# A new order for the first 250 of 1101 steps of a gated SSM-convolution and MLP-mixer kernel on one core

## The chip, the core and the metric

The kernel runs on one core of one Trainium2 chip. The metric is the device time of the whole program in microseconds (us). The kernel before took 228.67 us, the median of three runs (228.26 to 228.98).

The engines of the core are named as the profile names them: PE (TensorE, matmuls; PEld its weight loads), DVE (VectorE), ACT (ScalarE), POOL (GpSimd) and SP (SyncE, which here only issues DMAs). Each works through its own instruction queue in order.

## What is computed

All tensors are bf16; S = 2048 rows, D = 640 columns, F = 1536.

```python
g = sigmoid((x * gate_w).sum(-1))                     # x = A_q
k_shift = sum(k_pad[t:t+S] * shift_k[:, 3-t] for t in range(4))
kv = k_shift * v
y = causal_convolution_by_fft(kv, ssm_k) + kv * ssm_D
a = x * y
h = gelu(layernorm(x) @ w1)
hs = concat(shift(h[:, :160], +1), shift(h[:, 160:320], -1),
            shift(h[:, 320:480], +2), shift(h[:, 480:], -2)) @ w2
x1 = x + hs
b = x1 + gelu(layernorm(x1) @ w3) @ w4
out = g * a + (1 - g) * b
```

## The kernel before, in words

**Layout.** The 2048 rows lie as 128 partitions of 16 rows each (t = 0 to 15), cut in four chunks of four rows t. A chunk of x, k or v is 128 x 2560 bf16, 640 KB. The columns come in five blocks of 128.

**Order.** Every engine's instructions are written out by hand: ORDER is a list of 1101 names such as `mlp1.0.2:1`. The name is a function with its arguments, the number behind the colon is the step of it that is emitted (a generator's next part, or an element of a list of closures). So the list gives each engine its queue, and each queue is simply the list's steps for that engine in the list's order. Letters at the end of a name (`AVA`) say for each part whether ACT (A) or DVE (V) does the evacuation. SLOTS is the second hand-written table: for each ring of buffers (`c`: the eight PSUM banks; `row`: four buffers of a chunk; `gt`, `gq`, `xt` and others) it lists which buffer each allocation gets.

**The stage that the change touches**, up to the first matmul of w2 (`w2.0:0`, step 250):

- `warm` (L224): 23 matmuls of zeros. `consts0`, `pow0`, `row_order` (L220 to L255): constants, a first power on POOL, and the row list for gathers. `f4_table`, `f1_table`, `t2_table` (L280 to L325): sine tables; their arguments are made on DVE, the sine is taken on ACT, and t2_table's part 1 adds a 128 x 1024 table on POOL (L322).
- `load_x0`, `load_x` (L189 to L193), `load_w1` by halves (L195), `k_load.c:0` (L562): loads on SP's queue. `v_load.c` (L575): a gather of v's chunk c on POOL's queue (L173), into KV.
- `x_stats.c` (L667): sums for the layer norm, by bn_stats on DVE (V, L686) or by a Square and a Copy pass on ACT (A, L680 and L682), then scalars on DVE and the reciprocal root on POOL (L658). `x_norm.c` (L629) scales the rows. `x_turn.c` turns the chunk: by PE transposes with evacuations (letters; L620, L361 or L363) for chunks 0 and 1, by one transposing DMA (D, L653) for chunks 3 and 2.
- `k_load.c:1` to `:6`: the same transposes for k, in three banks (two of 8 blocks, one of 4), into KT; odd numbers are PE, even ones the evacuation. `k_wrap` (L567) makes the last three rows of KT again, shifted by a partition.
- `mlp1.c.u` (L701): five matmuls of 128 x 512 for chunk c and column group u, then Gelu on ACT. u = 0 and 1 need W1's first half, 2 and 3 the second, 4 the mixed columns that `w1_mixed` copies. `h_shift.c` (L750): copies on POOL for the row shifts.
- `tap.k` (L578): 76 matmuls that give k_shift of column block k in four PSUM banks; then for each quarter e the product with v: V is one DVE product straight from PSUM (L606), A a copy to yk on ACT (L600) and a product on DVE (L603). Each quarter's product takes all 16 rows of KV.
- `step1.KV.c` (L411): the first transform of a chunk of kv, five pairs of matmuls (L424), ten evacuations, two sends to DRAM on SP (L438). Each matmul reads only the column blocks that it covers. `load_h` (L178) loads ssm_k, `h_transpose` turns it.

From step 250 on follow w2, the rest of the transforms, w3 and w4, and the output.

Of the kernel before, what the change touches and what calls it, by code (L numbers as in the profile page):

```python
# [41 lines left out]
def kernel(  # L42
# [837 lines left out]
    def step4(t1, ev):  # L880
# [91 lines left out]
        "x_norm.1.VVVV:2 "
        "v_load.2:0 "
        "k_load.0.AAV:0 "
        "f1_table:1 "
        "mlp1.0.2:0 "
        "mlp1.0.3:0 "
        "x_norm.1.VVVV:3 "
        "v_load.0:0 "
        "k_load.1.AVV:0 "  # L980
        "k_load.2.VAV:6 "
        "mlp1.0.0:0 "
        "load_x.2:0 "
        "x_stats.3.VVAA:2 "
        "x_turn.1.VVV:0 "
        "x_turn.1.VVV:4 "
        "mlp1.0.1:0 "
        "x_stats.3.VVAA:3 "
        "x_turn.1.VVV:1 "
        "k_load.2.VAV:4 "  # L990
        "x_stats.3.VVAA:4 "
        "x_stats.3.VVAA:5 "
        "k_load.0.AAV:3 "
        "x_turn.1.VVV:5 "
        "mlp1.0.3:1 "
        "x_stats.3.VVAA:6 "
        "x_turn.1.VVV:2 "
        "v_load.3:0 "
        "x_turn.1.VVV:3 "
        "k_load.1.AVV:3 "  # L1000
        "w1_mixed:0 "
        "v_load.1:0 "
        "mlp1.0.0:1 "
        "x_stats.2.VVAA:0 "
        "mlp1.0.2:1 "
        "k_load.0.AAV:1 "
        "mlp1.0.1:1 "
        "x_stats.3.VVAA:7 "
        "k_load.0.AAV:5 "
        "mlp1.1.2:0 "  # L1010
        "x_norm.3.VVVV:0 "
        "x_norm.3.VVVV:1 "
        "k_load.0.AAV:4 "
        "load_cj:0 "
        "k_load.0.AAV:2 "
        "mlp1.1.2:1 "
        "x_norm.3.VVVV:2 "
        "x_norm.3.VVVV:3 "
        "x_stats.2.VVAA:1 "
        "k_load.1.AVV:5 "  # L1020
        "mlp1.0.4:0 "
        "k_load.1.AVV:4 "
        "mlp1.0.4:1 "
        "k_load.1.AVV:1 "
        "d_fold:0 "
        "mlp1.1.4:0 "
        "x_turn.3.D:0 "
        "kv_consts:0 "
        "x_stats.2.VVAA:2 "
        "mlp1.1.0:0 "  # L1030
        "k_load.2.VAV:2 "
        "k_wrap:0 "
        "k_load.1.AVV:6 "
        "mlp1.1.4:1 "
        "k_load.0.AAV:6 "
        "x_stats.2.VVAA:3 "
        "t2_table:0 "
        "load_w2:0 "
        "mlp1.1.3:0 "
        "k_load.1.AVV:2 "  # L1040
        "tap.3.VAVA:0 "
        "mlp1.1.0:1 "
        "x_stats.2.VVAA:4 "
        "h_shift.1:0 "
        "mlp1.1.3:1 "
        "tap.4.VAAV:0 "
        "x_stats.2.VVAA:5 "
        "tap.3.VAVA:1 "
        "tap.3.VAVA:3 "
        "tap.3.VAVA:5 "  # L1050
        "h_shift.0:0 "
        "mlp1.1.1:0 "
        "tap.4.VAAV:7 "
        "x_stats.2.VVAA:6 "
        "tap.3.VAVA:4 "
        "tap.4.VAAV:1 "
        "load_h.2:0 "
        "tap.3.VAVA:7 "
        "z_cols:0 "
        "mlp1.1.1:1 "  # L1060
        "load_gw:0 "
        "tap.4.VAAV:5 "
        "tap.4.VAAV:3 "
        "mlp1.3.1:0 "
        "tap.3.VAVA:2 "
        "x_stats.2.VVAA:7 "
        "x_norm.2.AVVV:0 "
        "mlp1.3.1:1 "
        "mlp1.3.4:0 "
        "tap.4.VAAV:2 "  # L1070
        "mlp1.3.0:0 "
        "x_norm.2.AVVV:1 "
        "tap.4.VAAV:8 "
        "x_norm.2.AVVV:2 "
        "x_norm.2.AVVV:3 "
        "h_shift.0:1 "
        "tap.4.VAAV:6 "
        "tap.3.VAVA:6 "
        "mlp1.3.4:1 "
        "tap.4.VAAV:4 "  # L1080
        "mlp1.3.0:1 "
        "tap.2.AVAA:0 "
        "x_turn.2.D:0 "
        "h_shift.3:0 "
        "tap.0.AVAA:0 "
        "tap.2.AVAA:3 "
        "tap.2.AVAA:7 "
        "tap.2.AVAA:5 "
        "tap.3.VAVA:8 "
        "mlp1.3.3:0 "  # L1090
        "tap.0.AVAA:3 "
        "h_shift.0:2 "
        "tap.0.AVAA:5 "
        "tap.2.AVAA:8 "
        "h_shift.3:1 "
        "mlp1.3.2:0 "
        "tap.0.AVAA:4 "
        "tap.2.AVAA:6 "
        "tap.0.AVAA:1 "
        "mlp1.3.3:1 "  # L1100
        "tap.0.AVAA:6 "
        "tap.1.VAVA:0 "
        "tap.0.AVAA:7 "
        "tap.1.VAVA:5 "
        "tap.1.VAVA:1 "
        "tap.2.AVAA:4 "
        "mlp1.3.2:1 "
        "load_h.1:0 "
        "mlp1.2.2:0 "
        "tap.0.AVAA:8 "  # L1110
        "tap.2.AVAA:1 "
        "tap.1.VAVA:7 "
        "h_shift.1:1 "
        "tap.0.AVAA:2 "
        "load_h.3:0 "
        "mlp1.2.3:0 "
        "tap.1.VAVA:2 "
        "tap.1.VAVA:3 "
        "tap.2.AVAA:2 "
        "step1.KV.3.AAAVAVAAAV:9 "  # L1120
        "tap.1.VAVA:8 "
        "tap.1.VAVA:6 "
        "mlp1.2.2:1 "
        "mlp1.2.3:1 "
        "tap.1.VAVA:4 "
        "step1.KV.3.AAAVAVAAAV:11 "
        "step1.KV.3.AAAVAVAAAV:3 "
        "step1.KV.3.AAAVAVAAAV:10 "
        "step1.KV.3.AAAVAVAAAV:12 "
        "h_shift.0:3 "  # L1130
        "step1.KV.3.AAAVAVAAAV:13 "
        "step1.KV.3.AAAVAVAAAV:5 "
        "mlp1.2.4:0 "
        "step1.KV.3.AAAVAVAAAV:6 "
        "load_h.4:0 "
        "step1.KV.3.AAAVAVAAAV:0 "
        "step1.KV.3.AAAVAVAAAV:4 "
        "step1.KV.3.AAAVAVAAAV:14 "
        "h_shift.1:2 "
        "step1.KV.2.AVAVAVAAAA:6 "  # L1140
        "z_rows:0 "
        "z_rows:1 "
        "step1.KV.3.AAAVAVAAAV:2 "
        "step1.KV.3.AAAVAVAAAV:7 "
        "load_h.0:0 "
        "step1.KV.1.VAVAAAVVAA:0 "
        "step1.KV.3.AAAVAVAAAV:8 "
        "step1.KV.2.AVAVAVAAAA:8 "
        "step1.KV.3.AAAVAVAAAV:1 "
        "step1.KV.2.AVAVAVAAAA:3 "  # L1150
        "z_rows:2 "
        "mlp1.2.1:0 "
        "mlp1.2.1:1 "
        "h_shift.3:2 "
        "step1.KV.3.AAAVAVAAAV:16 "
        "step1.KV.1.VAVAAAVVAA:1 "
        "step1.KV.3.AAAVAVAAAV:15 "
        "mlp1.2.0:0 "
        "load_w4.0:0 "
        "load_w4.2:0 "  # L1160
        "h_transpose.0.VV:2 "
        "step1.KV.2.AVAVAVAAAA:5 "
# [905 lines left out]
```

## Time and profile before

| | us |
|---|---|
| three runs | 228.26, 228.67 (median), 228.98 |
| the profiled execution | 229.4 |
| its span, first to last instruction | 227.6 |
| busy: PE, PEld | 217.3, 121.4 |
| busy: DVE, ACT, POOL | 185.1, 171.6, 37.8 |
| DMA moved over the span | 57.61 MB, mean 253 GB/s |

A row of the profile names a line of the kernel, an engine, an operation, and `out<-in` by the program's names; `x` is a count. In rows of groups, busy us and mean ns of one stand behind the bar, then the idle time of the engine just before them and what ended it. In rows of the timeline the first two numbers are start and length in us from the span's start. In the chain of waits each piece is start, length, engine, tile and line. A DMA's row ends with the us from its issue to its landing. The granted PE clock was 1.00 in every stage quoted.

### The profile page before, as it was taken

The numbers are of one execution on the slowest core, as the hardware profiler recorded it, in microseconds if no ns is written. First come the engines' busy times: TensorE is split into PE (matmuls) and PEld (weight loads), VectorE is DVE, ScalarE is ACT, GpSimd is POOL, SyncE is SP. The second block draws the span as 40 slices with busy tenths as digits, with TensorE's granted clock in tenths as the row PEclk, the third lists the DMA queues.
The fourth block names the chain that finished last, engine by engine and source line by source line (L and its number), as shares of the span: only waits on it lengthen the run. The fifth ranks groups of instructions, "written<-read, shape, count | busy, mean of one in ns | idle before, by whom it ended". The sixth has DMA issues, their size and how long they took to land.

```text
span 227.6 us, 6057 instructions
## 1 busy us (share of the span) xinstructions
PE 217.3 (95%) x2428; PEld 121.4 (53%) x2428; DVE 185.1 (81%) x447; ACT 171.6 (75%) x341; POOL 37.8 (17%) x91
## 2 busy tenths in 40 slices
PE   8989988799999997999999999999999999999994
PEld 3647545337855553334665544555533547657762
DVE  7999996977889968981899997989999941439994
ACT  4999986869899978999987597976989450266450
POOL 4247247806000331300510000000000000000000
PEclk9999999999999999999999999999999999999999
DMA  6999999888999899997799590593694779418915
GB/s 247 398 386 306 265 259 162 256 340 292 384 350 411 285 206 287 347 397 232 252 147 370 134 260 17 127 334 121 78 313 172 234 264 365 196 29 322 319 75 183
DMA packets 41802, 57.61 MB, mean 253 GB/s; under 512 B 18478, under 2 KB 34478, under 8 KB 41518
## 3 DMA queue, kind: packets, MB, share of 16 engines
q1 hardware_dynamic: 41198, 54.60, 76.8%
q0 software_dynamic: 576, 2.62, 3.3%
q8 instruction: 19, 0.31, 0.6%
q14 instruction: 9, 0.07, 0.1%
HBM read 34.93 MB, written 18.35 MB: 234 GB/s over the span
## 4 chain that ended last, share of the span: by engine, by line
PE 73%; ACT 14%; DMA 6%; DVE 4%; issue 1%; ACTq 0%
PE ps L868 23%; PE ps L841 22%; PE psm L708 5%; PE psw L789 5%; PE ps L466 4%; PE ps L894 4%; ACT stg L361 4%; DMA S_h<-stg 3%; PE ps L513 3%; PE ps L424 2%; ACT HT L711 2%; PE pst L391 2%; DMA S_x<-stg 2%; ACT KT L361 1%; PE psk L591 1%
## 5 line engine op out<-in xcount | busy, mean ns | idle before, releaser
L841 PE MATMUL ps<-x1t,W 128*128 128x512 bf16 x240 | 56.1, 380 | 0.1
L868 PEld LDWEIGHTS <-gt 128*128 128x128 bf16 x384 | 36.2, 98 | 17.8 <-issue 3.0
L845 ACT ACTIVATE gt<-ps 128x512 bf16<-128x512 f32 x48 | 27.6, 609 | 19.0 <-PE ps L868 10.6
L841 PEld LDWEIGHTS <-W 128*128 128x128 bf16 x240 | 21.8, 98 | 28.2 <-issue 5.5
L361 ACT CAST stg<-ps 128x512 bf16<-128x512 f32 x55 | 28.8, 608 | 5.3 <-PE ps L424 3.4
L868 PE MATMUL ps<-W4a,gt 128*128 128x320 bf16 (+2 forms) x160 | 27.1, 300 | 0.0
L868 PE MATMUL ps<-W4b,gt 128*128 128x320 bf16 (+2 forms) x160 | 27.0, 300 | 0.0
L871 DVE SCALAR_TENSOR_TENSOR X<-ps,OMG,X 128x320 bf16<-128x320 f32 (+2 forms) x32 | 17.2, 547 | 11.9 <-PE ps L868 11.7
L789 PE MATMUL psw<-WP,HT 128*128 128x320 bf16 x116 | 21.4, 300 | 1.3 <-ACT stg L361 1.3
L361 ACT CAST gs<-ps 128x320 bf16<-128x320 f32 x41 | 15.6, 440 | 8.8 <-PE ps L513 4.8
L708 PE MATMUL psm<-xt,WN 128*128 128x512 bf16 x80 | 19.1, 380 | 1.8 <-ACT xt L361 0.9
L363 DVE CAST XS<-ps 128x512 bf16<-128x512 f32 x19 | 12.5, 685 | 6.9 <-PE ps L466 6.9
L363 DVE CAST stg<-ps 128x512 bf16<-128x512 f32 x25 | 15.9, 684 | 2.1 <-PE ps L424 2.1
L361 ACT CAST hs<-ps 128x512 bf16<-128x512 f32 x28 | 15.0, 605 | 1.4 <-PE ps L466 1.4
L792 DVE SCALAR_TENSOR_TENSOR X<-psw,X 128x320 bf16<-128x320 f32 x32 | 14.5, 487 | 1.7 <-PE psw L789 1.5
L789 PEld LDWEIGHTS <-HT 128*128 128x128 bf16 x116 | 10.7, 98 | 8.1 <-issue 4.4
L898 ACT ACTIVATE y<-ps,GS 128x320 bf16<-128x320 f32 x22 | 10.4, 526 | 5.7 <-PE ps L894 3.5
L711 ACT ACTIVATE HT<-psm 128x512 bf16<-128x512 f32 x20 | 11.9, 616 | 3.1 <-PE psm L708 2.9
L868 PE MATMUL ps<-W4c,gt 128*128 128x320 bf16 (+2 forms) x64 | 13.9, 299 | 0.0
L708 PEld LDWEIGHTS <-WN 128*128 128x128 bf16 x80 | 7.5, 97 | 10.7 <-issue 1.3
L363 DVE CAST gs<-ps 128x320 bf16<-128x320 f32 x23 | 10.7, 485 | 2.4 <-PE ps L513 1.7
L789 PE MATMUL psw<-WP,HM 128*128 128x320 bf16 x44 | 12.3, 299 | 0.0
(155 smaller groups left out, 378.1 us busy)
## 6 DMA issues: line engine op xcount, KB each, us to landing
S_x<-stg SPq DMA_DIRECT2D x8, 640.0 KB, 4.3
S_h<-stg SPq DMA_DIRECT2D x8, 640.0 KB, 6.5
ax<-S_x SPq DMA_DIRECT2D x8, 640.0 KB, 7.8
ax<-S_h SPq DMA_DIRECT2D x8, 640.0 KB, 5.8
S_g<-gs SPq DMA_DIRECT2D x8, 640.0 KB, 3.5
kn<-in_A_k_dram SPq DMA_DIRECT2D x4, 640.0 KB, 5.0
E<-in_A_ssm_k_dram SPq DMA_DIRECT2D x5, 512.0 KB, 7.0
q<-in_A_q_dram SPq DMA_DIRECT2D x4, 640.0 KB, 4.6
```

Source lines behind the costliest of these rows:

```text
L361: A.copy(out=dst, in_=src)
L363: V.tensor_copy(out=dst, in_=src)
L466: PE.matmul(ps[j][q:q + 32, lo - 512 * u:hi - 512 * u], lhsT=CMP[HALF[j], 8 * b + 4 * h + i, c, :], rhs=st[name, 2 * b + h][HALF[j], i, lo ...
L708: PE.matmul(ps[:].rearrange("p (a b) -> p a b", a=4), lhsT=W1N[:, k, 160 * u:160 * u + P] if u < 4 else W1M[:, k, :], rhs=xt[:, :, k, :], ...
L711: A.activation(out=st["HT"][:, 4 * c:4 * c + 4, u, :], in_=ps[:].rearrange("p (t b) -> p t b", t=4), func=ACT.Gelu_apprx_tanh)
L789: PE.matmul(ps[:], lhsT=h_tile(f, t1), rhs=W2P[:, f, o:o + W], start=(f == 0), stop=(f == 4))
L792: V.scalar_tensor_tensor(out=X1[:, t1, o:o + W], in0=box["ps"][:], scalar=1.0, in1=X[:, t1, o:o + W], op0=ALU.mult, op1=ALU.add, accum_out ...
L841: PE.matmul(ps[:].rearrange("p (a b) -> p a b", a=4), lhsT=st["W3"][:, k, f * P:(f + 1) * P], rhs=xt[:, :, k, :], start=(k == 0), stop=(k ...
L845: A.activation(out=st["gt", c, f // 4][:, f % 4, :], in_=ps[:], func=ACT.Gelu_apprx_tanh)
L868: PE.matmul(ps[:], lhsT=st["gt", c, f // 4][:, f % 4, i * P:(i + 1) * P], rhs=st["W4", f // DC][:, f % DC, o:o + w], start=(f == 0), stop= ...
L871: V.scalar_tensor_tensor(out=X1[:, t1, o:o + w], in0=box["ps"][:], scalar=OMG[:, t1:t1 + 1], in1=X1[:, t1, o:o + w], op0=ALU.mult, op1=ALU ...
L898: A.activation(out=box["y"][:], in_=box["ps"][:], func=ACT.Copy, scale=GS[:, t1:t1 + 1])
```

## The change

ORDER gets a new beginning: the first 250 steps are the same set, apart from letters, in a new order; all steps behind them keep their order. What is new in it:

- The 23 warm matmuls come in one run. Two of the four gathers of v, v.2 and v.1, stand at the front of POOL's queue, ahead of the first statistics' reciprocal root; v.0 stands behind that of x_stats.1, and v.3 behind `h_shift.0:0`, which reads the Gelu of `mlp1.0.4`. Before, the four stood one behind the other after x_stats.1's.
- On SP's queue the order was x.0, k.3, x.1, k.2, x.3, W1's second half, its first, k.0, k.1, x.2. It is now x.0, k.3, x.1, x.3, W1's first half, its second, k.0, k.2, k.1, x.2. `load_h.3` goes from its place behind `load_h.1` to behind the two sends of step1.KV.3; `load_h.2` from ahead of x_turn.2 to behind it.
- The Sine of `f1_table:1` goes from ahead of all Gelus to behind most of them. `t2_table:0` goes from ahead of the products to among them.
- The taps come in the order 4, 3, 1, 0, 2 instead of 3, 4, 2, 0, 1; the first of them starts behind seven groups of mlp1, where it was nine.
- Letters: x_norm.0 VVAA to VVVA; x_turn.1 VVV to AAV; k.0 AAV to AVA, k.1 AVV to VVA, k.2 VAV to AVA; tap.3 VAVA to VVAV, tap.4 VAAV to VVAA, tap.2 AVAA to VVAV, tap.0 AVAA to AVVV, tap.1 VAVA to VAAV; step1.KV.3 AAAVAVAAAV to AAVVAVVAVA; step1.KV.1 and KV.2 each have one V turned to A.
- SLOTS for `c`, `gt`, `row` and `gq` are written anew for it.

For comparison, the old queues of PE (from the first transposes to the first matmul of step1) and of POOL, without letters:

```
PE:   k.3:1 k.3:5 warm:4 k.3:3 x_turn.0:0 k.2:5 k.2:1 x_turn.0:2 x_turn.0:4 k.2:3 mlp1.0.2 mlp1.0.3 mlp1.0.0
      x_turn.1:0 x_turn.1:4 mlp1.0.1 k.0:3 x_turn.1:2 k.1:3 k.0:1 k.0:5 mlp1.1.2 k.1:5 mlp1.0.4 k.1:1 mlp1.1.4
      mlp1.1.0 mlp1.1.3 tap.3 tap.4 mlp1.1.1 mlp1.3.1 mlp1.3.4 mlp1.3.0 tap.2 tap.0 mlp1.3.3 mlp1.3.2 tap.1
      mlp1.2.2 mlp1.2.3 step1.KV.3:9
POOL: consts0:0 pow0 x_stats.0:6 row_order x_stats.1:5 v.2 v.0 v.3 v.1 x_stats.3:7 h_shift.1:0 h_shift.0:0 z_cols:0
      x_stats.2:7 h_shift.0:1 h_shift.3:0 h_shift.0:2 h_shift.3:1 h_shift.1:1 h_shift.0:3 h_shift.1:2 z_rows:0
      h_shift.3:2 t2_table:1
```

The new beginning:

```diff
+        "open.L1.left:0 open.A2.right:0 consts0:0 warm:0 kv_alloc:0 warm:1 warm:2 warm:3 consts0:1 pow0:0 "
+        "f4_table:0 load_x0.0:0 warm:4 x_stats.0.VVVA:0 row_order:0 v_load.2:0 load_x0.1:0 x_stats.0.VVVA:1 "
+        "x_stats.0.VVVA:2 x_stats.0.VVVA:3 f4_table:1 x_stats.0.VVVA:4 x_stats.0.VVVA:5 v_load.1:0 k_load.3.AVA:0 "
+        "x_stats.0.VVVA:6 load_x.1:0 k_load.3.AVA:5 k_load.3.AVA:1 k_load.3.AVA:3 k_load.3.AVA:6 k_load.3.AVA:2 "
+        "f1_table:0 x_norm.0.VVVA:0 x_norm.0.VVVA:1 x_stats.1.VVVV:0 load_x.3:0 x_norm.0.VVVA:2 x_norm.0.VVVA:3 "
+        "x_turn.0.AAA:0 x_turn.0.AAA:1 load_w1.0:0 x_turn.0.AAA:4 x_turn.0.AAA:5 x_turn.0.AAA:2 x_turn.0.AAA:3 "
+        "load_w1.1:0 x_stats.1.VVVV:1 x_stats.1.VVVV:2 k_load.0.AVA:0 mlp1.0.0:0 x_stats.1.VVVV:3 x_stats.3.VVAA:0 "
+        "k_load.2.AVA:0 k_load.1.VVA:0 x_stats.3.VVAA:1 x_stats.1.VVVV:4 x_stats.3.VVAA:2 mlp1.0.2:0 "
+        "x_stats.3.VVAA:3 x_stats.3.VVAA:4 w1_mixed:0 x_stats.3.VVAA:5 x_stats.3.VVAA:6 mlp1.0.3:0 mlp1.0.0:1 "
+        "x_stats.1.VVVV:5 x_norm.1.VVVV:0 x_norm.1.VVVV:1 x_norm.1.VVVV:2 mlp1.0.3:1 k_load.0.AVA:5 k_load.0.AVA:6 "
+        "k_load.0.AVA:1 k_load.0.AVA:3 k_load.0.AVA:2 v_load.0:0 mlp1.0.2:1 mlp1.0.4:0 load_cj:0 z_cols:0 "
+        "x_stats.3.VVAA:7 mlp1.0.4:1 h_shift.0:0 k_load.2.AVA:5 k_load.2.AVA:6 x_turn.1.AAV:0 x_turn.1.AAV:1 "
+        "k_load.3.AVA:4 x_norm.1.VVVV:3 d_fold:0 k_wrap:0 k_load.2.AVA:3 x_turn.1.AAV:2 x_turn.1.AAV:3 load_x.2:0 "
+        "x_norm.3.VVVV:0 k_load.1.VVA:5 x_norm.3.VVVV:1 x_norm.3.VVVV:2 x_norm.3.VVVV:3 mlp1.0.1:0 k_load.1.VVA:3 "
+        "mlp1.0.1:1 k_load.2.AVA:4 x_turn.1.AAV:4 k_load.0.AVA:4 k_load.2.AVA:1 k_load.2.AVA:2 v_load.3:0 "
+        "k_load.1.VVA:1 x_turn.1.AAV:5 kv_consts:0 mlp1.1.4:0 x_turn.3.D:0 k_load.1.VVA:2 k_load.1.VVA:4 mlp1.1.0:0 "
+        "k_load.1.VVA:6 x_stats.2.VVAA:0 tap.4.VVAA:0 tap.4.VVAA:3 tap.4.VVAA:1 x_stats.2.VVAA:1 x_stats.2.VVAA:2 "
+        "mlp1.1.3:0 mlp1.1.4:1 x_stats.2.VVAA:3 x_stats.2.VVAA:4 load_gw:0 tap.4.VVAA:2 mlp1.1.0:1 x_stats.2.VVAA:5 "
+        "tap.4.VVAA:4 mlp1.1.2:0 tap.4.VVAA:7 x_stats.2.VVAA:6 tap.3.VVAV:0 tap.3.VVAV:1 tap.3.VVAV:3 tap.3.VVAV:4 "
+        "mlp1.1.2:1 tap.4.VVAA:5 tap.4.VVAA:6 tap.3.VVAV:5 x_stats.2.VVAA:7 x_norm.2.AVVV:0 x_norm.2.AVVV:1 "
+        "mlp1.3.0:0 x_norm.2.AVVV:2 x_norm.2.AVVV:3 tap.3.VVAV:2 mlp1.3.0:1 h_shift.1:0 tap.4.VVAA:8 mlp1.3.1:0 "
+        "mlp1.3.1:1 mlp1.3.4:0 mlp1.3.4:1 tap.3.VVAV:6 mlp1.1.3:1 mlp1.3.2:0 mlp1.3.2:1 h_shift.0:1 tap.1.VAAV:0 "
+        "tap.1.VAAV:5 load_w2:0 tap.3.VVAV:7 tap.3.VVAV:8 t2_table:0 tap.1.VAAV:3 tap.0.AVVV:0 tap.0.AVVV:1 "
+        "tap.0.AVVV:3 tap.1.VAAV:7 mlp1.1.1:0 tap.1.VAAV:8 x_turn.2.D:0 tap.0.AVVV:7 tap.1.VAAV:1 tap.1.VAAV:2 "
+        "f1_table:1 tap.2.VVAV:0 tap.2.VVAV:3 tap.0.AVVV:4 load_h.0:0 tap.2.VVAV:1 tap.0.AVVV:2 tap.1.VAAV:4 "
+        "z_rows:0 mlp1.1.1:1 tap.0.AVVV:8 load_h.2:0 tap.2.VVAV:5 tap.2.VVAV:7 load_h.4:0 tap.0.AVVV:5 mlp1.3.3:0 "
+        "mlp1.3.3:1 mlp1.2.3:0 mlp1.2.3:1 tap.2.VVAV:2 tap.2.VVAV:8 tap.0.AVVV:6 h_shift.0:2 tap.1.VAAV:6 "
+        "mlp1.2.2:0 h_shift.0:3 mlp1.2.2:1 tap.2.VVAV:4 tap.2.VVAV:6 step1.KV.3.AAVVAVVAVA:6 "
...
+        "h_transpose.0.VV:2 h_shift.3:0 h_shift.3:1 h_shift.3:2 w2.0:0 mlp1.2.4:1 mlp1.2.0:1 w2.15:0 t2_table:1 "
```

More of the change, by code (lines that the diff above doesn't have):

```diff
@@ L972 @@
[L972 to L1162, printed above, removed]
-        "w2.0:0 "
-        "mlp1.2.4:1 "
-        "mlp1.2.0:1 "
-        "w2.15:0 "
-        "t2_table:1 "
-        "step1.KV.2.AVAVAVAAAA:4 "
@@ L1236 @@
-        "step1.KV.0.VAAVAAAAAV:7 "
-        "w2.2:0 "
-        "w2.1:1 "
-        "step1.KV.0.VAAVAAAAAV:10 "
-        "step1.KV.0.VAAVAAAAAV:3 "
-        "h_shift.2:3 "
-        "step1.KV.0.VAAVAAAAAV:0 "
-        "h_shift.3:3 "
-        "w2.3:3 "
-        "step1.KV.0.VAAVAAAAAV:12 "
-        "w2.2:1 "
-        "step1.KV.0.VAAVAAAAAV:5 "
-        "step1.KV.0.VAAVAAAAAV:1 "
-        "step1.KV.2.AVAVAVAAAA:16 "
-        "step1.KV.0.VAAVAAAAAV:4 "
-        "step1.KV.0.VAAVAAAAAV:14 "
-        "swap.A2.C.right:0 "
```

903 lines of the change are left out of this document (8 added, 895 removed), and 140 rows, old and new, of the table ORDER.

## Prediction, made before the changed kernel was run

> **What bounds the kernel now.** I read the page's head first, then the busy time by stage (columns: stretch, its length, busy us of PE, PEld, DVE, ACT and POOL with their instructions, granted clock, DMA share, GB/s), then the chain of waits through the stage that the change touches.
>
> ```profile
> span 227.6 us, 6057 instructions
> ...
> PE 217.3 (95%) x2428; PEld 121.4 (53%) x2428; DVE 185.1 (81%) x447; ACT 171.6 (75%) x341; POOL 37.8 (17%) x91
> ```
> ```profile
> 26.95:45.36 18.41, 15.08 (x423) 8.73 (x423) 16.24 (x42) 14.86 (x29) 12.24 (x30) 1.00 0.93 221
> 31.90:43.04 11.14, 10.37 (x262) 5.96 (x261) 9.19 (x19) 9.12 (x17) 8.42 (x25) 1.00 0.90 223
> 45.36:52.25 6.89, 6.89 (x58) 2.83 (x58) 4.47 (x7) 4.51 (x9) 0.24 (x1) 1.00 0.88 350
> 52.25:84.00 31.75, 31.65 (x274) 20.39 (x273) 27.67 (x88) 29.51 (x58) 6.96 (x14) 1.00 1.05 331
> 84.00:100.00 16.00, 14.59 (x143) 6.34 (x141) 13.29 (x35) 14.43 (x31) 3.40 (x11) 1.00 0.93 312
> 100.00:223.60 123.60, 123.59 (x1343) 68.41 (x1341) 97.88 (x185) 84.78 (x178) 3.70 (x11) 1.00 0.69 211
> ```
>
> From 45.36 on TensorE is full but for 1.4 us in 84 to 100 and the last 4 us. The steps after the 250th are kept, so the question is only when TensorE gets to them: the first matmul of w2 (step 250) ran at 52.25. Before it, TensorE idled 3.3 us between 26.95 (first tap) and 45.36. The chain says what ended that stretch.
>
> ```profile
> 40.26 1.09 PE psk L591 x76
> 41.35 0.67 DVE KV L606
> ...
> 42.71 0.68 DVE KV L606
> 43.39 1.93 DVE KV L603
> ...
> 45.36 0.61 PE ps L424 x4
> ```
> ```profile
> 43.12 1.91 POOL L322 TENSOR_TENSOR n<-ab 128x1024 int32<-128x1024 int32 x1
> ```
> ```profile
> 43.31 2.00 DVE L603 TENSOR_TENSOR KV<-yk,KV 128x512 bf16<-128x512 bf16 x1
> ```
>
> The last of the 20 products of the taps with v ended the wait, at 45.32. It took 2.00 us where others of its form take 0.42 (below), and stood still while POOL's 1.91 us add for the t2 table ran. So the stage ends with the products, and its tail is an accident of two queues. I call the end of the last product T; T is 45.32 now. From T to w2 TensorE is busy 6.89 of 6.89 us on the same list in both orders. So the forecast is the new T.
>
> **The change, part by part.** Costs come from groups by form up to 52.3 us, and from single rows.
>
> ```profile
> L665 DVE TENSOR_SCALAR xn<-X,RS,NB 128x640 bf16<-128x640 bf16 x13 | 5.4, 468 | 0.3 <-POOL NB L659 0.2
> L606 DVE TENSOR_TENSOR KV<-psk,KV 128x512 bf16<-128x512 f32 x8 | 5.4, 683 | 0.8 <-PE psk L591 0.8
> ...
> L363 DVE COPY KT<-pst 128x1024 bf16<-128x1024 bf16 x3 | 2.0, 669 | 0.0
> ...
> L363 DVE COPY KT<-pst 128x512 bf16<-128x512 bf16 x3 | 1.1, 404 | 0.0
> ```
> ```profile
> 28.59 0.16 DVE L269 TENSOR_SCALAR sm<-BF 128x1 f32<-128x1 f32 x2
> ...
> 29.59 0.16 DVE L690 TENSOR_SCALAR MU<-s 128x2 f32<-128x2 f32 x1
> ...
> 30.27 0.42 DVE L603 TENSOR_TENSOR KV<-yk,KV 128x512 bf16<-128x512 bf16 x1
> ```
>
> *DVE up to the first product.* At 28.59 DVE had done all that stands ahead of the first product in the new order (the t2 table's scalars, 28.59 to 29.59, and those of x_stats.2, 29.59 to 30.27, now come behind it). New letters change this load: a third normalisation of chunk 0 on DVE, +0.42 (5.4/13); two large copies of xt less, taken at KT's 0.67 each, -1.34; five large copies of KT for three large and three small, +0.23. Sum -0.7: DVE is ready at 27.9.
>
> *The gathers of v.* Every product reads all 16 rows, so the first waits for the last of four gathers. Two move to the front of POOL's queue, where it sat idle for 4.39 us ahead of the first rstd (the row at 7.60 below; 2.5 us of issuing fit in it). But v.3 now stands behind h_shift.0:0, and so behind the Gelu of mlp1.0.4 on ACT.
>
> ```profile
> 11.22 2.41 ACT L361 COPY xt<-pst 128x1024 bf16<-128x1024 bf16 x3
> ```
> ```profile
> 17.02 0.74 ACT L682 ACTIVATE jk<-X 128x640 bf16<-128x640 bf16 x1
> ...
> 17.87 1.28 ACT L711 ACT_TABLE_LOAD   x1
> 19.16 2.06 ACT L711 ACTIVATE HT<-psm 128x512 bf16<-128x512 f32 x4
> ```
> ```profile
> 7.60 1.02 POOL L658 TENSOR_TENSOR RS<-VE,EXPO 128x4 f32<-128x4 f32 x1 [4.39 <-DVE pf L261]
> ```
> ```profile
> 15.64 1.22 POOL L173 DMA_INDIRECT KV<-in_A_v_dram,ROWS  x1 [0.18 <-issue]
> ...
> 19.65 0.94 POOL L173 DMA_INDIRECT KV<-in_A_v_dram,ROWS  x1 [0.30 <-issue]
> ...
> 26.00 1.41 POOL L762 COPY HM<-HT 32x512 bf16<-32x512 bf16 x2 [3.97 <-ACT HT L711]
> ```
> ```profile
> KV<-in_A_v_dram,ROWS POOLq DMA_INDIRECT x1, 6.4
> ```
> ```profile
> KV<-in_A_v_dram,ROWS POOLq DMA_INDIRECT x2, 7.3
> ```
>
> xt.0 was whole on ACT at 13.63 (11.22 + 2.41); with one normalisation less ahead of it I take 13.1. Then four Square and Copy passes of x_stats.3 (0.85 from 17.02 to 17.87), 3.4; the table load, 1.28; four Gelus up to mlp1.0.4's at 0.515, 2.06; two copies of KT, large and small, some 1.5. The Gelu is done at 21.3 and the shift copy, 0.7, at 22.0; the gather goes out at 22.1, where the last one went at 19.65 before (landing about 27.0). Landing took 6.4 us for the first and up to 7.3 for the last; so 28.5 to 29.4, and I take 29.0. The early gathers thus buy nothing: the first product goes from DVE's 27.9 to 29.0, since what counts is the last gather.
>
> *From the first product to the last.* Codes turn five tap quarters from A to V: 13 products straight from PSUM at 0.675 (5.4/8) and seven from yk at 0.42, 11.7 us; scalars of x_stats.2, 0.68; three normalisations, 1.25; t2 scalars, 1.0. Sum 14.6, so 43.6. The second tap needs two banks that its forerunner's products free at 29.0 + 2 x 0.675 = 30.35, and takes 1.09 us on TensorE, to 31.45; DVE has the scalars until 31.05, and waits 0.4. T would be 44.0, were it not for the add.
>
> *POOL's add.* It comes behind the rstd of x_stats.2 and all shifts up to h_shift.3:2.
>
> ```profile
> 30.45 1.11 POOL L658 TENSOR_TENSOR RS<-VE,EXPO 128x4 f32<-128x4 f32 x1 [2.90 <-DVE VE L696]
> 31.64 0.20 POOL L659 TENSOR_TENSOR NB<-MU,RS 128x4 f32<-128x4 f32 x1
> ```
>
> The rstd runs 1.4 us, 31.05 to 32.5. Then the same 25 pieces as between 31.90 and 43.04 (8.42 busy, 11.14 with gaps) and one copy of 0.7 more: the add starts between 41.6 and 44.3. I take 42.5, near the busy sum, since the Gelus that POOL waited for are older by then. The last three products are tap.1:6 (from 42.5), tap.2:4 (from PSUM) and tap.2:6 (from 43.6). The add starts with or just behind the first and holds the third until 44.4 to 44.8. **T is 45.05**, 0.27 before the old one; the bounds are 44.0 (missed) and 45.9 (add caught whole).
>
> *TensorE's own queue.*
>
> ```profile
> 26.96 0.23 PE L591 MATMUL psk<-DG,KT 32*128 32x128 bf16 x3
> ...
> 37.93 2.33 PE L708 MATMUL psm<-xt,WN 128*128 128x512 bf16 x10
> ```
>
> From the first tap (26.96 less DVE's 0.7, since the tap waits for its last copy of KT) to the first matmul of step1.KV.3: five taps at 1.09 and ten groups of mlp1 at 1.13, 16.75 us, where the old order had eight groups; and the bank wait, 0.75. It gets there at 43.75. So T cannot fall below 43.75, and up to 45.05 there is 1.3 us of cover.
>
> *W1 and k.* W1's halves move ahead of three chunks of k on SP's queue, and two gathers of 640 KB run beside them.
>
> ```profile
> WN<-in_B_w_dram SPq DMA_DIRECT2D x1, 400.0 KB, 9.1
> ```
> ```profile
> WN<-in_B_w_dram SPq DMA_DIRECT2D x1, 400.0 KB, 10.0
> ```
>
> Issued at 3.54 and about 4.05, they landed at 12.6 and 14.05 with 3600 and 4000 KB of the queue moved. Now 2960 KB end with the first half: 10.5 if the gathers take nothing, 14.0 if all their 1280 KB go before it. xt.0 is due at 13.1, so mlp1 starts between 13.1 and 14.0; the 1.3 us above cover it. [...]
>
> *ACT.*
>
> ```profile
> L600 ACT CAST yk<-psk 128x512 bf16<-128x512 f32 x12 | 6.6, 605 | 1.3 <-PE psk L591 1.3
> ```
>
> f1's Sin moves behind the first Gelus, which adds a switch to its table and one back, 2.57 us by the load's row; five copies of yk fall away (6.6/12 = 0.55 each), 2.75. ACT idles 3.55 us in 26.95 to 45.36. The yk of tap.2 comes behind both loads, near 42.2, and is due at 43.6: cover 1.4. [...]
>
> *Behind step 250.*
>
> ```profile
> 58.26 3.24 PE L391 MATMUL pst<-IDB,E 128*128 128x128 bf16 x48
> ```
>
> load_h.3 goes behind two sends: one load of 512 KB more in a stretch with a DMA share of 0.88. Its transposes came from 58.26 on; the sends can leave some 3 us behind T, so the load goes out near 49 and has 9 us. I take 0; an estimate of up to 0.5 more stands for a full queue.
>
> **Sum:** -0.27 us. The profiled execution took 229.4 us around a span of 227.6, so it would be 229.1; against the median of 228.67 this is **228.4**. A measurement of this kernel tells 0.3%, 0.69 us, from no change.
>
> **The rivals.**
> *The add misses the products.* If it starts after 43.6, or ends by 42.5, T is 44.0 or little above: -1.3 us, 227.35. Any hold below 0.63 us counts here. For it: the add's start is known to 2.7 us only. Against: its window of harm, 40.6 to 43.6, holds my estimate.
> *The last gather comes late: slower.* All of DVE's products, and through the rstd POOL's add too, move one for one with the landing of v.3. Slower than before by 0.69 us from a landing at 29.96 on; at 31.0 it is +1.7, 230.4. For it: x_turn.3 is on the DMA engines just then, and every late Gelu is paid in full. Against: nothing in the trace landed later than 7.3 us after its issue.
> [...]
> *mlp1 starts late.* If W1 comes at 16 or later, TensorE reaches T's place after 46: 229.5 and up. It idles then for over 2 us ahead of mlp1; the clock, granted at 1.00 in every stage above, might fall.
>
> **How the numbers follow.** Forecast 0.33; missed add 0.33; late gather 0.20; table switches 0.07; late mlp1 0.07. Faster by over 0.3%: 0.33; within: 0.33; slower: 0.34. The range takes in the missed add with TensorE's floor (43.75, 227.1) and the late gather to 31.0: 227.0 to 230.5. The likeliest case alone: 227.98 to 229.36.
>
> **What would show it.** Right: v.3 issued near 22 and landed near 29, the first product right behind; the add in L322 starting near 42.5 with one L603 stretched to over 1 us; L424 waiting for DVE near 45. Wrong: TensorE, not DVE, last at L424; products starting before 28; ACT waiting in its table loads with yk late.

## The result, and the profile after

The changed kernel took 232.22 us (median of four runs, 231.25 to 232.72), the kernel before 228.82 in the same comparison: a ratio of 1.0145, 95% interval 1.0103 to 1.0187. Slower by some 3.3 us, where 228.4 was forecast and the range ended at 230.5. The profiled execution took 231.25. Ratios and intervals, here and below, leave out executions more than 1.5% above the fastest of the same kernel, which the medians include, so a ratio is not the quotient of two medians.

The page's head of the changed kernel, then its busy time by stage (the columns as before; the sixth pair is granted clock and DMA share, the last number GB/s):

```profile
span 229.5 us, 6056 instructions
...
PE 218.5 (95%) x2427; PEld 121.5 (53%) x2428; DVE 185.2 (81%) x445; ACT 173.0 (75%) x340; POOL 38.4 (17%) x91
```
```profile
10.00:20.00 10.00, 5.44 (x27) 2.34 (x26) 9.03 (x34) 8.44 (x15) 3.81 (x6) 0.83 1.07 383
15.50:20.60 5.10, 5.10 (x18) 2.02 (x19) 4.30 (x18) 3.00 (x6) 3.55 (x6) 0.67 1.04 387
...
26.95:45.36 18.41, 18.34 (x445) 10.46 (x443) 17.20 (x45) 16.78 (x31) 10.51 (x28) 1.00 0.75 207
45.36:52.25 6.89, 5.21 (x45) 1.59 (x44) 5.70 (x7) 4.82 (x11) 2.15 (x2) 1.00 0.52 207
...
84.00:100.00 16.00, 15.86 (x141) 7.17 (x140) 13.46 (x42) 15.16 (x31) 4.74 (x11) 1.00 1.08 305
```

The stretch ahead of the taps, which the prediction did not look at by stage, in the kernel before:

```profile
10.00:20.00 10.00, 8.82 (x92) 5.98 (x90) 9.69 (x35) 9.94 (x19) 4.65 (x6) 1.00 1.05 351
```

The loss is made here: between 10 and 20 us TensorE was busy 5.44 us instead of 8.82, and its clock was 0.83 of full. Behind 20 us it has no hole left until 45.36 (18.34 of 18.41, where it idled 3.3 before): it is behind and never catches up. At 46.25 it has to wait for the last product all the same, 1.7 us. The chain of waits through the stage (start, length, what) names the order of it:

```profile
3.05 12.40 DMA WN<-in_B_w_dram
15.45 0.05 issue
15.50 5.11 PE psm L708 x15
20.61 0.02 issue
20.63 0.60 ACT HT L711
21.23 1.39 ACT KT L361 x2
22.62 1.00 ACT HT L711 x2
23.62 0.06 issue
23.68 0.60 POOL HM L762
24.28 0.18 issue
24.46 7.03 DMA KV<-in_A_v_dram,ROWS
...
45.96 1.93 DVE KV L603
```

W1's first half landed at 15.45, 12.4 us after its issue; three groups of mlp1 took 5.11 us; then the Gelu of mlp1.0.4 (done at 23.62), the shift copy, and v.3, issued at 24.46 and landed at 31.49. T is 47.89, 2.57 behind the old 45.32.

That the time follows T holds for all 17 executions profiled for this document, those of the experiments included: T lies between 44.20 and 58.58 in them, and the span less T between 181.3 and 182.4 us.

TensorE's rows at that place, first of the kernel before, then of the changed one (the bracket is the idle time ahead and its releaser):

```profile
13.19 3.67 PE L708 MATMUL psm<-xt,WN 128*128 128x512 bf16 x15 [0.90 <-ACT xt L361]
```
```profile
15.50 5.10 PE L708 MATMUL psm<-xt,WN 128*128 128x512 bf16 x15 [3.56 <-DMA WN<-in_B_w_dram]
```

What was on the DMA engines while W1 was awaited: the transfers of the changed kernel from 10 to 12 us (queue: packets, MB, time as a share of 16 engines).

```profile
DMA packets 308, 0.82 MB, mean 412 GB/s; under 512 B 22, under 2 KB 165, under 8 KB 308
...
q0 software_dynamic: 154, 0.71, 85.4%
q1 hardware_dynamic: 154, 0.12, 17.5%
```

The gathers (q0) and the loads (q1) had the same number of packets, 154 each (78 and 80 from 10 to 11 us, 76 and 74 from 11 to 12), but 0.71 MB against 0.12. So by the counts the two queues moved packet for packet in this stretch, and a gather's packet carries 4.6 KB where one of the loads' carries 0.8 on average. What equal counts do to a load of small packets the prediction had not asked. All of the two gathers' 1.31 MB had moved by 14.0.

From T on, 1.27 us come back where TensorE idled 1.41 us before and 0.14 now (84 to 100), and some 0.6 are lost in small pieces that I did not follow; the span grew by 1.9. Against the earlier profile (229.4) the execution shown is 1.9 longer; the median of runs moved by more, since the old profile lay 0.7 above its median and the new one 1.0 below.

### The profile page after: what moved, and what is told of

It is laid out like the page before. It is cut to its first block, busy times and chain, and to the rows that moved or that the text cites. A ratio compares the mean times of both kernels' runs of the same rounds, so it can differ in the third digit from the quotient of the medians.

```text
span 229.5 us, 6056 instructions
## 1 busy us (share of the span) xinstructions
PE 218.5 (95%) x2427; PEld 121.5 (53%) x2428; DVE 185.2 (81%) x445; ACT 173.0 (75%) x340; POOL 38.4 (17%) x91
## 4 chain that ended last, share of the span: by engine, by line
PE 72%; DMA 11%; DVE 10%; ACT 2%; POOL 2%; issue 1%; SPq 1%; DVEq 0%; POOLq 0%; ACTq 0%
PE ps L841 23%; PE ps L868 23%; PE psw L789 7%; DMA WN<-in_B_w_dram 5%; PE ps L466 5%; PE ps L894 4%; DVE KV L606 3%; DMA KV<-in_A_v_dram,ROWS 3%; PE ps L513 3%; PE ps L424 3%; PE psm L708 3%; DMA S_x<-stg 2%; PE pst L391 2%; DVE X L792 2%; DVE KV L603 2%
## 5 line engine op out<-in xcount | busy, mean ns | idle before, releaser
L708 PE MATMUL psm<-xt,WN 128*128 128x512 bf16 x80 | 20.5, 405 | 3.6 <-DMA WN<-in_B_w_dram 3.6
L711 ACT ACTIVATE HT<-psm 128x512 bf16<-128x512 f32 x20 | 11.4, 604 | 3.0 <-PE psm L708 3.0
L798 ACT ACTIVATE jk<-X 128x640 bf16<-128x640 bf16 x16 | 12.1, 759 | 0.2 <-DVE X L792 0.2
```

Of the source, the lines that this page charges most:

```text
L708: PE.matmul(ps[:].rearrange("p (a b) -> p a b", a=4), lhsT=W1N[:, k, 160 * u:160 * u + P] if u < 4 else W1M[:, k, :], rhs=xt[:, :, k, :], ...
L711: A.activation(out=st["HT"][:, 4 * c:4 * c + 4, u, :], in_=ps[:].rearrange("p (t b) -> p t b", t=4), func=ACT.Gelu_apprx_tanh)
L798: A.activation(out=jk[:], in_=X1[:, t1, :], func=ACT.Square, accum_out=S12[:, 1, t1:t1 + 1])
```

## Experiments

Theory: two gathers in front of W1 make W1 late, TensorE idles and its clock falls to half (0.50 from 16 to 19 us in the changed kernel), and Gelu, v.3 and products follow. Rivals: the late gather v.3 alone; W1's own place in the queue; the half clock alone. All ratios are to the kernel before, run beside each, with 95% intervals; a point is 1% of its time.

**e1: both early gathers back.**

```diff
- row_order:0 v_load.2:0 load_x0.1:0
+ row_order:0 load_x0.1:0
- x_stats.0.VVVA:5 v_load.1:0 k_load.3.AVA:0
+ x_stats.0.VVVA:5 k_load.3.AVA:0
- k_load.0.AVA:2 v_load.0:0
+ k_load.0.AVA:2 v_load.2:0 v_load.1:0 v_load.0:0
```

> The changed kernel with the gathers v.2 and v.1 put back behind the reciprocal root of x_stats.1, just ahead of v.0; v.3 stays behind h_shift.0:0. Theory (the early gathers hold W1's first half back, TensorE waits 3.56 us for it and then runs three groups at half clock): W1's first half lands near 11, the first mlp1 starts near 13.4 at clock 1.00, the Gelu of mlp1.0.4 ends 2.07 earlier, v.3 lands near 29.4, the last product ends near 45.8, and the time is 228.0 to 229.0. Rival (W1 is late for its own place in SP's queue, not for the gathers): mlp1 still starts after 15 and the time stays within 0.7 of the changed kernel's, 231.5 to 232.9.

Measured 231.21 (1.0083, 1.0049 to 1.0117). Stages and TensorE's row:

```profile
10.00:13.90 3.90, 1.39 (x22) 1.10 (x20) 3.80 (x12) 3.90 (x6) 0.00 (x0) 0.96 1.08 387
13.90:18.82 4.92, 4.92 (x18) 1.97 (x18) 4.12 (x20) 4.80 (x10) 2.85 (x4) 0.68 0.90 320
```
```profile
13.90 4.92 PE L708 MATMUL psm<-xt,WN 128*128 128x512 bf16 x15 [1.45 <-ACT xt L361]
```

W1 is no longer what TensorE waits for; the wait is for ACT's copy of xt.0. That part of the theory holds, and W1's own place is out. But the clock fell all the same (0.68 over the groups), after 1.39 us of work in 3.90; the transposes of k.2, which filled this gap in the kernel before (2.84 us of work in the 3.90 ahead of mlp1, clock 1.00), now stand behind mlp1. The time came down by 0.6 points instead of the expected 1.4, with T at 47.06 where 45.8 was expected.

The later experiments bear out the first part. With both gathers in front of the new order the groups started between 14.48 and 16.55 in six executions (the changed kernel, e2, e3, e5, r1, s3); with one or none in front they started between 13.29 and 13.97 in eight (e1, e7, e8, r2 to r4, s1, s2).

**e2: v.3 alone forward.**

```diff
- k_load.2.AVA:2 v_load.3:0 k_load.1.VVA:1
+ k_load.2.AVA:2 k_load.1.VVA:1
- k_load.0.AVA:2 v_load.0:0
+ k_load.0.AVA:2 v_load.0:0 v_load.3:0
```

> The changed kernel with v.3 alone moved forward, from behind h_shift.0:0 to right behind v.0. Theory (all queues are late by W1, so the late gather costs only the 0.41 us that DVE waits for it): v.3 is issued near 18 and lands near 25, the first product moves from 31.61 to 31.2, and the time falls by 0.4 at most, to 231.8. Rival (the late gather is the cause, as the prediction's slow case had it): the time falls by 2 or more, to 230 or below.

Measured 231.14 (1.0096, 1.0066 to 1.0126). The first product:

```profile
31.76 1.29 DVE L606 TENSOR_TENSOR KV<-psk,KV 128x512 bf16<-128x512 f32 x2
```

It did not move from 31.61, though v.3 was issued at 18.31: DVE, whose copies of KT are late through TensorE, gets there no sooner. T was 48.04, no earlier than 47.89. So the gather's place is not the cause while W1 is late: two paths lead from the late start to the first product, one through v.3 and one through TensorE and DVE, and they differ by less than half a microsecond. The ratio lies a little below the changed kernel's interval (from 1.0103 on), but the two intervals overlap, and the profile shows no gain.

**e3 and s3: TensorE kept busy while W1 is awaited** (matmuls of zeros into the bank that the first group then overwrites; 12 in e3, 8 in s3).

```diff
+        for i in range(12 if (c, u) == (0, 0) else 0):
+            PE.matmul(ps[:].rearrange("p (a b) -> p a b", a=4), lhsT=WZ[:], rhs=WZ[:].unsqueeze(1).to_broadcast([P, 4, P]), start=True, stop=True)
```

> The changed kernel with twelve matmuls of zeros in front of the first mlp1 group, in its own bank, so that TensorE does not idle while W1 is awaited (the result is not touched: the first real matmul overwrites the bank). W1 stays as late. Theory (the half clock costs a part of its own): the clock stays at 1.00, the three groups of mlp1 take 3.7 us where they took 5.1, the products start about 1.4 earlier, and the time is 230.8; runs with two throttled stretches vanish, so the median may gain up to 2. Rival (only the late W1 counts, the half clock is hidden behind ACT's work): no change, 231.5 to 232.9.

> The changed kernel (W1 late, v.2 and v.1 in front, add in its place) with eight matmuls of zeros ahead of the first mlp1 group, where e3_bridge had twelve. Theory (the half clock costs a part of its own, and e3's gain went into two gaps of 1.03 and 1.36 us in TensorE's queue, in the middle of its groups, that waited for nothing the profile shows): with another place of the queue's cuts the gaps shrink, the products start 1.0 to 1.4 earlier, ratio 1.008 to 1.012. Rival (the half clock is covered and e3 was no accident): ratio 1.0145 or more.

Measured 233.4 (1.0206, 1.0144 to 1.0269) and 231.84 (1.0130, 1.0078 to 1.0182). e3, then s3:

```profile
16.16 3.41 PE L710 MATMUL psm<-xt,WN 128*128 128x512 bf16 x15 [1.22 <-DMA WN<-in_B_w_dram]
...
34.75 0.17 PE L591 MATMUL psk<-DG,KT 32*128 32x32 bf16 x1 [1.03 <-issue]
...
45.40 2.97 PE L710 MATMUL psm<-xt,WN 128*128 128x512 bf16 x13 [1.36 <-issue]
```
```profile
16.55 3.48 PE L710 MATMUL psm<-xt,WN 128*128 128x512 bf16 x15 [2.58 <-DMA WN<-in_B_w_dram]
```

The three groups are back at 3.4 to 3.5 us, at a clock of 1.00 from 10 to 26.95 in both executions, but no time is gained: W1 landed later in both, and two gaps stand in the middle of TensorE's groups, waiting for nothing that the profile shows (2.4 us in e3, 1.1 in s3; with four matmuls fewer ahead of them, s3's stand four matmuls later in the list). In e3 the groups ended at 19.57 instead of 20.60, and v.3 went out a microsecond earlier, at 23.44; but it took 7.8 us to land, and the first product came only 0.3 earlier, at 31.33. Inconclusive for the price of the half clock.

**e4: the same two gathers in front of the old order.**

```diff
- x_stats.0.VVVA:6 warm:4 row_order:0 k_load.2.VAV:0
+ x_stats.0.VVVA:6 warm:4 k_load.2.VAV:0
- kv_alloc:0 k_load.3.AVA:0
+ kv_alloc:0 row_order:0 v_load.2:0 v_load.1:0 k_load.3.AVA:0
```

> The kernel before with two gathers alone moved forward (v.2 and v.1, right behind the row list and ahead of the first reciprocal root); all else as before. Theory (gathers in front take the DMA engines from the loads): W1's halves land 2.5 to 3.3 later than at 12.6 and 14.05, TensorE waits over 3 us ahead of mlp1, the clock falls to half for 3.4 us, and the time is 1.5 to 3.5 over the kernel before, 230.2 to 232.2. Rival (the early gathers are harmless by themselves): within 0.7 of the kernel before.

Measured 231.23 (1.0089, 1.0049 to 1.0130): the gathers alone cost 2.0 us. TensorE's waits (total, times, longest) and its row:

```profile
PE pst L620 <- DMA kn<-in_A_k_dram: 3.8, 2, 2.5
```
```profile
17.58 5.22 PE L708 MATMUL psm<-xt,WN 128*128 128x512 bf16 x15 [1.83 <-ACT F L278]
```

The size is as expected, the loads are others: k.2, which is due first, came late, and then x.3 (13.3 us from its issue to 16.36), since ACT's Sine that TensorE waits for stands behind a pass over it. mlp1 started 4.4 us later than at 13.19. W1 was late as well: the first weight load for it waited 2.1 us and also began at 17.58.

**e5 and e6: POOL's add later**, in the changed kernel (e5) and the one before (e6).

```diff
- w2.15:0 t2_table:1
+ w2.15:0
- h_shift.2:1
+ h_shift.2:1 t2_table:1
```

> The changed kernel with t2_table:1 (POOL's add of the t2 table and the DVE step behind it) moved from behind w2.15:0 to behind h_shift.2:1, so that the add runs after the products of the taps. Theory (the add holds the last product by some 1.6 us and is one of the terms of T): the last L603 takes 0.42 where it took 2.00, T goes from 47.89 to 46.3, TensorE's own arrival at 46.25 is the next bound, and the time falls by 1.6, to about 230.6. Rival (late W1 alone sets the time and the add is hidden): no change, 231.5 to 232.9.

> The kernel before with t2_table:1 moved in the same way, behind h_shift.2:1. Theory (T is the tail that the two queues make by accident): the last L603 takes 0.42, T goes from 45.32 to 43.8, TensorE waits under 0.2 for it where it waited 1.5, and the time falls by 1.0 to 1.5, to about 227.4. Rival (the 1.5 us come back behind w2, where TensorE idles 1.4 us in 84 to 100, or the add now holds the shifts that w2 needs): within 0.5 of the kernel before.

e5: 230.29 (1.0067, 1.0028 to 1.0105). e6: 228.89 (1.0007, 0.9979 to 1.0036). The first and the last product of e5:

```profile
32.66 1.29 DVE L606 TENSOR_TENSOR KV<-psk,KV 128x512 bf16<-128x512 f32 x2 [1.73 <-DMA KV<-in_A_v_dram,ROWS]
...
46.92 0.41 DVE L603 TENSOR_TENSOR KV<-yk,KV 128x512 bf16<-128x512 bf16 x1
```

The last product of e6, and two pieces of its chain of waits:

```profile
45.68 0.60 DVE L603 TENSOR_TENSOR KV<-yk,KV 128x512 bf16<-128x512 bf16 x1
```
```profile
14.45 3.41 PE psm L708 x15
...
33.92 1.84 issue
```

In the changed kernel the product fell from 2.00 to 0.41 us and the ratio by 0.8 points, with intervals that just touch: the add is a term there (s1 below shows it more clearly). T fell only to 47.33, not to the expected 46.3, since v.3 took 8.3 us to land in this execution and the first product came a microsecond later than 31.61.

In the old one the product shrank too, and nothing was gained; T was 46.28, later than 45.32. In the execution shown the stage itself came late: mlp1 waited for W1 and started at 14.45 instead of 13.19, a gap of 1.8 us stood in a group of TensorE, of the same kind as in e3, and the first product came at 32.37 instead of 30.27. The edit touches none of this. Why the median of e6's twelve runs shows no gain either stays open.

**e7 and e8: gathers back, v.0 behind the root of x_stats.3, add late; e8 with six matmuls of zeros.**

```diff
- k_load.0.AVA:2 v_load.0:0 mlp1.0.2:1
+ k_load.0.AVA:2 v_load.2:0 v_load.1:0 mlp1.0.2:1
- x_stats.3.VVAA:7 mlp1.0.4:1
+ x_stats.3.VVAA:7 v_load.0:0 mlp1.0.4:1
```

> The changed kernel with three edits: v.2 and v.1 back behind the reciprocal root of x_stats.1; v.0 behind that of x_stats.3, so that this root isn't held by three gathers; and t2_table:1 behind h_shift.2:1. TensorE still idles 2.5 us between 10.5 and 13.9, because the transposes of k.2, which the kernel before ran there, stand behind mlp1. Theory (W1, the half clock and the add are three terms that add up): x_turn.3 is issued near 23.4 instead of 24.3, the clock falls to half once more, T is 45.5 to 46.3, and the time 229.0 to 230.0. Rival (what is left is not in this stage): it stays at the 231 of the kernel with the gathers back alone.

> The kernel of e7_gathers_back_add_late with six matmuls of zeros ahead of the first mlp1 group, in its bank, to fill 1.4 of the 2.5 us that TensorE idles there. Theory (the half clock is a term of its own once nothing else is late): the clock stays at 1.00, the three groups of mlp1 take 3.7 us where they take 4.9, T falls by up to 1.2 and the time to about 228.5, level with the kernel before. Rival (the half clock is covered, since ACT's Gelus and the transposing DMA of chunk 3 set the pace): same time as without the bridge, within 0.4.

Measured 239.31 (1.0420, 1.0361 to 1.0480) and 240.03 (1.0393, 1.0335 to 1.0450): no theory had this. DMAs issued from 23 to 25 us (the last number is the time to landing), e7, then the changed kernel:

```profile
KV<-in_A_v_dram,ROWS POOLq DMA_INDIRECT x1, 18.4
xt<-xn SPq DMA_TRANSPOSE x1, 19.1
```
```profile
xt<-xn SPq DMA_TRANSPOSE x1, 6.9
KV<-in_A_v_dram,ROWS POOLq DMA_INDIRECT x1, 7.0
```

The gather of v.3, issued at 23.56, and the transposing DMA of x_turn.3, issued at 23.61, took some 19 us each, and the first product waited for v.3 until 42.06. e8 shows the same (18.3 and 19.3 us). The number of gathers in flight is not the reason. v.0 was in flight too, and landed after 7.1 us. In the kernel before, e1, e2 and r3 the transposing DMA also started with two or more gathers in flight, and took 8.0, 9.5, 5.0 and 9.0 us; e1's:

```profile
24.30 9.46 DMA xt<-xn
```

One thing that e7 and e8 alone have is that the gather and the transposing DMA were issued 0.05 us apart; in the other executions 0.7 us or more lay between them. No run tests whether that is the cause, and it stays open. (The execution shown of e7 took 242.06, the longest of its six; the shortest took 237.11.)

**r1 to r4: one gather back, and the repairs without e7's move.** r1 is the changed kernel again. r2 puts back v.1 alone (v.2 stays in front), r3 is e1 with e5's edit, r4 is r3 with six matmuls of zeros.

```diff
- x_stats.0.VVVA:5 v_load.1:0 k_load.3.AVA:0
+ x_stats.0.VVVA:5 k_load.3.AVA:0
- k_load.0.AVA:2 v_load.0:0
+ k_load.0.AVA:2 v_load.1:0 v_load.0:0
```

> The changed kernel once more, as a common mark for the kernels beside it on this chip. Every theory: a ratio of 1.012 to 1.017 to the kernel before, the first mlp1 near 15.4, the first product near 31.6.

> The changed kernel with v.1 alone put back ahead of v.0; v.2 stays at the front. Theory (bytes in front of W1 set its landing): 640 KB at some 0.41 MB per us are 1.6 us, so W1's first half lands near 13.9 instead of 15.45, xt.0 is ready near 13.4, the first mlp1 starts near 13.9, and the time lies at the level of the kernel with both gathers back, a ratio of 1.007 to 1.010. Rival (one gather in front is enough, by the alternation of the two queues): W1 still lands after 15 and the ratio stays at 1.012 or more.

> The changed kernel with v.2 and v.1 back ahead of v.0 (v.0 in its place) and t2_table:1 behind h_shift.2:1. Theory (W1's lateness and the add are separate terms): the gathers back gave 0.6% and the late add 0.8%; together 1.2% at least, a ratio of 1.000 to 1.004, T near 46.1, since TensorE's first groups still run at half clock. Rival (TensorE's own queue is the floor, as it reaches step1.KV.3 only near 46.2): the second edit adds nothing, 1.007 to 1.010.

> The kernel of r3_gathers_back_add_late_2 with six matmuls of zeros ahead of the first mlp1 group in its own bank. Theory (the half clock is a term of its own): the clock stays at 1.00, the three groups take 3.7 us where they take 4.9, TensorE reaches step1.KV.3 by 45, and the ratio falls by 0.3 to 0.5% below that of r3, to 0.996 to 1.000. Rival (chunk 3's transposing DMA, which held TensorE to 33.80 with the gathers back, takes the gain): same ratio as r3 within 0.2%.

Measured: r1 231.46 (1.0158, 1.0105 to 1.0212), r2 229.95 (1.0106, 1.0046 to 1.0166), r3 229.34 (1.0044, 1.0018 to 1.0069), r4 229.63 (1.0056, 1.0027 to 1.0084). r1's groups started at 14.48, a microsecond earlier than the changed kernel's, and T was 47.88 again. The profiled execution of r2, the shortest of its six (228.34), comes out at the prediction's numbers:

```profile
13.32 3.40 PE L708 MATMUL psm<-xt,WN 128*128 128x512 bf16 x15 [1.46 <-ACT xt L361]
```
```profile
28.81 1.29 DVE L606 TENSOR_TENSOR KV<-psk,KV 128x512 bf16<-128x512 f32 x2
...
43.34 1.53 DVE L603 TENSOR_TENSOR KV<-yk,KV 128x512 bf16<-128x512 bf16 x1
```
```profile
42.60 1.98 POOL L322 TENSOR_TENSOR n<-ab 128x1024 int32<-128x1024 int32 x1
```

W1 in time at full clock (1.00 in this execution) gives a first product at 28.81, the add at 42.60, T at 44.87. The five other runs of r2 had clocks of 0.985 to 0.993 and took 229.0 to 232.1. And the way to these numbers is not the prediction's. v.3 landed at 27.8, 5.6 us after its issue; the first product came a microsecond later, when DVE was done with the statistics of x_stats.2. The chain that ends in r2's T runs through the transposing DMA of chunk 3 and the groups of mlp1 that read it:

```profile
22.95 8.83 DMA xt<-xn
...
31.82 4.49 PE psm L708 x20
```

r3 took away the early gathers and the held product, and lies 1.1 points below r1, clear of the noise; how this splits (0.6 from e1, 0.4 more from the add) is not, since the intervals of e1 and r3 overlap. r4 restored the clock (0.998 to 1.000 in nine of its twelve runs, where r3's twelve had 0.990 to 0.998) and gained nothing: with both gathers back the chains of r3 and of r4 run through the same transposing DMA. TensorE's wait in r4:

```profile
33.66 2.33 PE L710 MATMUL psm<-xt,WN 128*128 128x512 bf16 x10 [1.17 <-DMA xt<-xn]
```

**s1 and s2: r2 with the add late, without and with six matmuls of zeros.**

> The changed kernel with v.1 back ahead of v.0 (v.2 stays in front) and t2_table:1 behind h_shift.2:1. In the profile of the kernel with one gather back W1 came in time (TensorE waited for ACT's last copy of xt.0 alone), the clock was 1.00 and T 44.87, with the last L603 at 1.53 us. Theory (the add is a term of its own): the last L603 takes 0.42, T falls to 43.8, and the ratio is 0.4 to 0.6% below the 1.0106 of one gather back, 1.004 to 1.007. Rival (the spread of that kernel, 228.34 to 230.15, comes from the clock alone and the add is covered): no change, 1.009 or more.

> The same with six matmuls of zeros ahead of the first mlp1 group in its own bank. Theory (half clock is a term of its own once W1 is in time and no gather stands in front of chunk 3's root): all runs have the clock at 1.00, as the one at 228.34 had, and the time is 227.0 to 228.2, at or below the kernel before: a version that beats both. Rival (as with both gathers back, the clock recovered gives nothing): the ratio of s1 within 0.2%.

Measured 227.60 (0.9976, 0.9937 to 1.0016) and 227.88 (0.9975, 0.9953 to 0.9998). The last product of s1 and the first groups of s2:

```profile
43.79 0.41 DVE L603 TENSOR_TENSOR KV<-yk,KV 128x512 bf16<-128x512 bf16 x1
```
```profile
13.61 3.46 PE L710 MATMUL psm<-xt,WN 128*128 128x512 bf16 x15 [0.28 <-DMA WN<-in_B_w_dram]
```

T is 44.20 in s1. Its ratio lies 1.3 points below r2's, more than the theory's 0.6, and the two intervals do not meet: the add is a term. s2 is the one version with its whole interval (its longest run left out) below the kernel before, by a quarter of a per cent at the middle. The two ratios are equal, so the clock's recovery shows only in the spread: eleven runs of s2 had clocks of 0.997 to 1.000 and took 226.9 to 228.4, and one at 0.978 took 239.3; in s1 seven at 1.00 took 226.9 to 227.6, and five at 0.978 to 0.993 took 229.6 to 235.8.

## Why the prediction was wrong, point by point

- *W1 and k: the step that failed.* It let W1's first half land between 10.5 and 14.0 and mlp1 start by 14.0; they came at 15.45 and 15.50. The bound was wrong by its own rows: 2960 and 1280 KB are 4240, 240 more than the 4000 that had landed at 14.05, which at the 351 GB/s of that stretch is 14.7, not 14.0. And of its two bounds the late one was no extreme but the case that came: with equal counts of packets (154 against 154 above), of 4.6 KB against 0.8, the gathers were through by 14.0, ahead of W1. The last 0.7 us are in neither count: 5.00 MB had moved when W1's first half landed, where 4240 KB are 4.34; the other 0.66 MB are loads queued behind it (0.52 at 14.05 in the kernel before), and what put them first was not followed.
- *Its price.* The 1.3 us of cover were TensorE's alone, up to T. The Gelu of mlp1.0.4 has no such cover: it releases v.3, and the prediction had worked out that chain with mlp1 never late. The Gelu was done at 23.62 instead of 21.3, and the slow rival, the late gather (one for one with T), came true by a cause that I had priced as another rival, late mlp1, with a chance of 0.07. Nor is that chain the only one: DVE, which the prediction had ready at 27.9, was ready at 31.2, and e2 shows that it sets the first product when v.3 is early.
- *The clock.* I noted that it might fall and gave it no size. The three groups took 5.10 us instead of 3.67, at a mean clock of 0.67 instead of 1.00, so end at 20.60; in r1 they started 1.0 earlier and ended at 20.41, because they took 5.93 (clock 0.50 from 14 to 16, 0.55 from 16 to 20). How much of the time the half clock costs by itself is not settled: where it was restored no run gained for sure.
- *First product.* 29.0 forecast, 31.61 measured; 28.81 in r2, with v.3 issued at 22.20 for the forecast 22.1. The nearness of 28.81 to 29.0 is luck: v.3 landed 1.2 us before the forecast, and DVE was ready 0.9 after it. The range of landings was also misread: 7.3 us is the median of two rows, and the last gather of the kernel before took 7.6.
- *First to last product.* Forecast 16.05 with the add and 15.0 without; measured 16.28 (changed), 16.06 (r2) and 15.24 (s1); with the add e1 took 16.90, without it e5 took 14.67. In r2 and s1 this stretch ends with the path through chunk 3's transposing DMA, for which the prediction has no term, so the agreement there is in part luck.
- *POOL's add.* Forecast to start at 42.5 and to hold one product; it started at 42.60 in r2, at 45.69 in the changed kernel, all else being late, and its product took 2.00 us. Without it the ratio was 0.8 points lower in e5 than in the changed kernel, and 1.3 lower in s1 than in r2.
- *TensorE's floor* of 43.75 became 46.25, 2.5 later, from W1.
- *Table switches.* No more than their loads (1.28 us each), as taken. ACT in the changed kernel:

```profile
41.11 1.28 ACT L278 ACT_TABLE_LOAD   x1
42.40 0.40 ACT L278 ACTIVATE F<-n,NPI 128x128 bf16<-128x128 int32 x1
42.82 1.28 ACT L711 ACT_TABLE_LOAD   x1
44.12 0.60 ACT L711 ACTIVATE HT<-psm 128x512 bf16<-128x512 f32 x1
```

The next operation begins 1.29 to 1.30 us after each load does, and the one before the second load ends 0.02 us ahead of it. Switches that cost more than their loads, to which the prediction gave a chance of 0.07, are not seen here.
- *Behind step 250.* load_h.3 was taken at 0, with 0.5 as a bound; in the chain of waits TensorE's block of 48 transposes of ssm_k came at 61.09 instead of 58.33, 2.76 later where T was 2.57 later. That the idle time in 84 to 100 would shrink by 1.27 was not foreseen.

So T decides the time, as forecast, and the stretch from the first product on had about the forecast length. That r2's profile took 228.34 for a forecast of 228.4 proves no more: it is the shortest of six runs of another kernel, and its chain is another. The error that made the changed kernel slower is in the first fifteen microseconds, in a transfer that I had bounded and not followed to its last reader.

## What to carry to other kernels

Idle time at the front of a gather's queue is no reason to issue it early: ask which load it displaces, and whose packets are larger (4.6 KB against 0.8 here). A late start is priced along every chain that leaves it, not along one engine's cover, and a hole in TensorE's work just ahead of it can cost the clock as well (here 0.67 over the 5.10 us behind a hole of 3.56). A total that comes out as forecast does not confirm its terms: read in the trace what released each step.
